# All eight weight tiles of the second product prepared in the first layer stage, with low parts on GpSimd

## The chip, the core and the metric

The kernel runs on one core of a Trainium2 chip. TensorE (PE) multiplies matrices into PSUM; VectorE (DVE), ScalarE (ACT) and GpSimd (POOL) do elementwise work; SyncE (SP) mostly issues DMAs. Each engine runs its own instructions in order, and semaphores order the engines against each other. The metric is the time of one execution on the device, in microseconds (us).

## What is computed

Attention with a learned bias, and then two feed-forward layers on its output, 2304 tokens by 512. The first layer is the one that matters here:

```python
attn = softmax(q @ k.T / 8 + bias) @ v          # 4 batches x 8 heads, 576 x 64
x = attn.transpose(0, 2, 1, 3).reshape(2304, 512)
h = x @ w_in                                     # first product, 512 -> 2048
x1 = (h * cos(h)) @ w_out                        # second product, 2048 -> 512
h2 = x1 @ w_in2
out = (max(h2, 0) + alpha * min(h2, 0)) @ w_out2
```

The weights come as 64-bit floats and are made into 32-bit floats on the chip.

## The kernel before

**Arithmetic.** A product keeps 32-bit accuracy by splitting each operand into a high part (rounded, `hi`) and a low part (`lo` = value - `hi`), and adding three products: hi by hi, hi by lo, lo by hi. So weights need a conversion (`conv`: two ScalarE copies of a 64-bit float's halves, two VectorE operations, one GpSimd addition) and a split (`split_to`: a ScalarE copy for the high part, a subtraction for the low part).

**Stages.** The bias and attention stages go through 16 pairs (two heads of one batch); `h_phase0` computes `h` and `h * cos(h)`; `o_phase(0)` the second product; `h_phase1` and `o_phase(1)` the second layer.

**Weight tiles of the first product.** `wi(0, f)` makes 16 of them (`f` 0 to 15), all in the attention stages: high and low parts on GpSimd; the first six stay on chip, the others go to memory (`w_d`) and are loaded again as `w` when `h_phase0` begins.

**Weight tiles of the second product.** It is done with seven products of half-size blocks in place of eight, so each of its eight tiles (`stage_wo(0, k)`) converts two blocks of 128 rows, forms combinations of them on VectorE (`ct`, named `wt` in the trace), and leaves four groups (`leave_w`) that serve the seven products p = 1; 5, 6; 3, 7; 2, 4. For k below `NIP` = 4 they are written into tiles that stay on chip (`wo`). For k = 4 to 7 each group is split into the tile `st` (`sw` in the trace), of which there is one buffer, and stored to memory (`w2_d`, also shown as `w_d`); `o_phase(0)` loads these as `W1[p]`. The copy of the next group has to wait until the store of the one before has landed.

**Who does what, when.** The attention's loop emits stages and counts them in `j`; a list `JOBS` of weight tiles is worked off beside it. A job starts when `j` has reached `WS0 + WSR * due`, and `due` grows by the cost of each, 1.0 for a `wi`, 3.0 for a `stage_wo`. The 16 `wi` come first, then `stage_wo(0, 4)` to `(0, 7)`; `stage_wo(0, 0)` to `(0, 3)` are done in `h_phase0`, at `H0R` = 2.6 steps for each of its units. In the attention the low parts of `split_to` are GpSimd's and the stores SP's; later the low parts are VectorE's and the stores GpSimd's. A scheduler then sets the order on each engine.

**The attention's own work.** Per pair, TensorE makes scores S; VectorE adds the bias and takes the maximum (L495); ScalarE takes exps in place (L508: `P`, and once in each pair `Pr`, for the last rows of both heads); TensorE transposes P (`T_A`, `T_B`), ScalarE and VectorE copy the transposes out of PSUM, and TensorE multiplies by v (`x_A`, `x_B`).

**The first layer stage.** `h_phase0` has 36 units, each with 24 products of 512 columns (or 48 of 256) into one of three PSUM tiles. `act1` then empties the tile: ScalarE `ta` (L818), VectorE two steps of the cosine's argument (L819, L820), ScalarE the sine (L822), VectorE the product with `h` (L823), which is the last reader of the PSUM tile.

Of the kernel before, what the change touches and what calls it, by code (L numbers as in the profile page):

```python
# [9 lines left out]
F32 = mybir.dt.float32  # L10
# [5 lines left out]
ALU = mybir.AluOpType  # L16
# [9 lines left out]
NK = NF // 2  # L26
# [11 lines left out]
HIA, LOP = 2, 1  # L38
UPB, EPB = {"D": 11, "A": 4}, 6
PBUF, BTB = 6, 10  # L40
FIRST, SIDE, SMOD, BFIRST, BRATE, SPL, WS0, WSR, PER = 4, 6, 2, 8, 2.5, 3, 28, 3.6, 1.0
SR = 2.0
NSP = 2
AHEAD = 3
# [6 lines left out]
NDIR = 6  # L51
XA, HX = 2, 300
RING, LO = 4, 3
NIP, H0R, H1R = 4, 2.6, 7.0
ORDS = ((1, 5, 6, 3, 7, 2, 4), (1, 5, 6, 3, 7, 2, 4))
GRPS = (((1,), (5, 6), (3, 7), (2, 4)), ((1,), (5, 6), (2, 3), (7, 4)))

# [16 lines left out]
def attn_mlp_kernel(ctx: ExitStack, tc: tile.TileContext, a: dict, out: bass.AP):  # L74
    nc = tc.nc
    ve, se, ge, te, sy = nc.vector, nc.scalar, nc.gpsimd, nc.tensor, nc.sync
# [97 lines left out]
    w2_d = [dr.tile([7, 128, NK, 2, 256], F32, tag=f"w2_d{i}", name=f"w2_d{i}") for i in range(2)]  # L174
    g_d = [dr.tile([NF, 128, NT], F32, tag=f"g_d{i}", name=f"g_d{i}") for i in range(2)]
    chunk = {}
    WO = {}
# [4 lines left out]
    pinned = []  # L182
# [16 lines left out]
    def hold(ins):  # L199
        if pinned:  # L200
            return behind(ins, anchor[-1]) if anchor else ins
        return behind(ins, exps[-1]) if FIRST in firsts else ins
# [42 lines left out]
    def halves_of(x):  # L245
        return x[:, 0:256], x[:, 256:512]

    def cols(x, n):
        return x.rearrange("p (n q) -> p n q", n=n)

    def split_to(hi, lo, w, eng=None):
        hold(se.activation(out=hi, in_=w, func=AF.Copy))
        yield
        hold((eng or (ve if pinned else ge)).tensor_tensor(out=lo, in0=w, in1=hi.bitcast(F32), op=ALU.subtract))
        yield

    PLACES = [{p: (g, i) for g, ps in enumerate(G) for i, p in enumerate(ps)} for G in GRPS]
# [1 line left out]
    def leave_w(layer, k, g, x):  # L259
        ps = GRPS[layer][g]  # L260
        n = len(ps)
        if (layer == 0 and k < NIP) or (layer == 1 and g < 3):
            w = WO[layer, g]
            yield from split_to(w[:, :, k, 0, :], w[:, :, k, 1, :], x)
            return
        st = wpool["t"].tile([128, 2, 2, 256], F32R, tag="st", name=f"sw{layer}_{k}_{g}")
        yield from split_to(st[:, 0:n, 0, :], st[:, 0:n, 1, :], x)
        for i, p in enumerate(ps):
            (ge if pinned else sy).dma_start(out=w2_d[layer][SLOT[p], :, k], in_=st[:, i].bitcast(F32))
        yield  # L270

    SLOT = {p: p - 1 for p in range(1, 8)}

    def stage_wo(layer, k):
        box = []
        yield from conv(layer, 2 * k, 1, box)
        yield from conv(layer, 2 * k + 1, 1, box)
        ct = wpool["t"].tile([128, 4, 256], F32, tag="ct", name=f"wt{layer}_{k}")
        sub = lambda o, u, v, op=ALU.subtract: hold(ve.tensor_tensor(out=o, in0=u, in1=v, op=op))
        c0, c1, c2, c3 = (ct[:, i] for i in range(4))  # L280
        u1, u2 = halves_of(box[0])
        v1, v2 = halves_of(box[1])
        if layer == 0:
            sub(c0, u2, v2, ALU.add)
            sub(c3, u1, u2)
            yield
            sub(c1, c0, u1)
            sub(c2, v1, c1)
            yield
            order = (cols(u1, 1), ct[:, 0:2], ct[:, 2:4], cols(box[1], 2))  # L290
        else:
            sub(c0, u2, u1)
            sub(c2, v2, u2)
            yield
            sub(c1, v2, c0)
            sub(c3, v1, c1)
            yield
            order = (cols(u1, 1), ct[:, 0:2], cols(box[1], 2), ct[:, 2:4])
        for g, x in enumerate(order):
            yield from leave_w(layer, k, g, x)  # L300
# [459 lines left out]
    W1 = {}  # L760
# [4 lines left out]
    def h_phase0():  # L765
# [5 lines left out]
        with ExitStack() as c:  # L771
# [65 lines left out]
            for f in range(NDIR, NF):  # L837
                wt[f] = wb[f - NDIR].tile([128, 2, 512], F32R, tag="w", name=f"w{f}")
                fetch(wt[f].bitcast(F32), w_d[f])
            fetch(W1[1].bitcast(F32), w2_d[0][SLOT[1], :, 4:8])  # L840
            bg.extend(stage_wo(0, k) for k in range(NIP))
            quota = 0.0
            for j, (t, f) in enumerate(units):
                ps = emit_h(t, f)
# [2 lines left out]
                if t + 1 < len(TILES):  # L847
                    with tc.high_priority(offset=XP):
# [4 lines left out]
                        if f in ((8, 12) if TILES[t][1] < TMAX else (XA + 4, XA + 6)):  # L853
                            k = 2 * (f in (12, XA + 6) and f != 8 or f == 8 and TILES[t][1] == TMAX)
# [227 lines left out]
    def h_phase1():  # L1082
        runs = [[(0, 512), (512, 1024)], [(1024, 1536), (1536, 2048)], [(2048, 2304)]]
        with ExitStack() as c:
# [6 lines left out]
            def x_prep(q):  # L1091
                x = X[q // 2][:, :, :, 2 * TS * (q % 2):2 * TS * (q % 2) + 2 * TS]
                for h in range(NCC):
                    if q < NSP:
                        ins = ge.dma_start(out=x[:, :, h].bitcast(F32), in_=x1_d[q][:, h].rearrange("l p i n -> p l (i n)"))
                        later(ins, last[0])
                        continue
                    (sy if q == 2 else ge).dma_start(out=x[:, 1, h].bitcast(F32), in_=x1_d[q][h].rearrange("p i n -> p (i n)"))
                yield
                for h in range(NCC if q >= NSP else 0):  # L1100
                    yield from split_to(x[:, 0, h], x[:, 1, h], x[:, 1, h].bitcast(F32))
                have.add(q)
# [141 lines left out]
```

## Time and profile before

| | |
|---|---|
| median of three runs | 1097.58 us (1096.16 to 1098.42) |
| the profiled execution | 1097.86 us, of which the span of its instructions 1096.0 |
| busy: TensorE, VectorE, ScalarE, GpSimd | 96%, 73%, 59%, 21% of the span |
| chain that ended last | TensorE 81%, DMA 6%, VectorE 6%, ScalarE 4%, GpSimd 1% |
| bytes moved | 216.09 MB, 197 GB/s in the mean |

The busy share is a mean over stages with different limits: which engine binds a stage is read from that stage's windows and from who waited for whom there. The chain is followed back from the last instruction, at each step to what released it.

### The profile page before, as it was taken

To read this page: it belongs to the slowest core of one execution; us is meant where nothing else is said; L and a number is where in the kernel's file an instruction comes from. 1 tells how busy PE (TensorE), PEld (TensorE's weight loads), DVE (VectorE), ACT (ScalarE), POOL (GpSimd) and SP (SyncE) were. 2 spreads that over 40 slices of the span, in tenths; PEclk is the share of its full clock that TensorE was granted. 3 is DMA by queue.
4 is the path that set the end of the run, shared out by engine and by line. 5 is a ranking of instruction groups with operands and counts; after the bars stand their busy time and mean duration, and the time that the engine had idled before them with its cause. 6 is when DMAs were issued, how large, how long until landed. Compare 5 with 4: busy or idle time off the path is not lost.

```text
span 1096.0 us, 18670 instructions
## 1 busy us (share of the span) xinstructions
PE 1055.6 (96%) x7024; PEld 891.4 (81%) x7024; DVE 802.1 (73%) x1296; ACT 642.8 (59%) x1076; POOL 225.5 (21%) x232
## 2 busy tenths in 40 slices
PE   6799999999789999999999999999999999999998
PEld 1246677777567889888899999988888889999998
DVE  7876787777675898878787777677756847777673
ACT  6996777887775565555454545466555544444442
POOL 0005675674343110010000000323222300000000
PEclk9999999999999999999999999999999999999999
DMA  8765748675448654336568172876655649554621
GB/s 322 221 171 161 220 138 270 197 218 188 154 138 304 247 195 163 135 135 227 216 205 305 47 250 70 322 263 226 221 203 185 223 164 361 158 198 130 216 73 44
DMA packets 105578, 216.09 MB, mean 197 GB/s; under 512 B 11280, under 2 KB 57104, under 8 KB 104080
## 3 DMA queue, kind: packets, MB, share of 16 engines
q1 hardware_dynamic: 75088, 154.07, 44.1%
q10 hardware_dynamic: 27968, 50.34, 12.2%
q0 software_dynamic: 2432, 10.49, 2.5%
q8 instruction: 55, 0.90, 0.4%
q14 instruction: 35, 0.29, 0.1%
HBM read 132.14 MB, written 82.72 MB: 196 GB/s over the span
## 4 chain that ended last, share of the span: by engine, by line
PE 81%; DMA 6%; DVE 6%; ACT 4%; issue 2%; POOL 1%; SPq 1%; ACTq 0%; POOLq 0%; DVEq 0%
PE h L809 18%; PE v L1139 18%; PE ob L1008 14%; PE oc L1008 9%; PE oa L1008 8%; PE S L479 5%; PE x_B L598 2%; PE T_A L573 2%; PE T_B L573 2%; DVE P L495 2%; PE x_A L598 2%; DMA w_d<-sw 1%; PE bps L142 1%; ACT be L156 1%; DMA bias_d<-be 1%
## 5 line engine op out<-in xcount | busy, mean ns | idle before, releaser
L1139 PE MATMUL v<-x,v 128*128 128x512 f32 (+1 forms) x984 | 198.0, 364 | 0.0
L1139 PEld LDWEIGHTS v<-x,v 128*128 128x128 f32 x984 | 168.5, 189 | 29.5
L809 PE MATMUL h<-xhi,w 128*128 128x512 f32 (+1 forms) x640 | 183.9, 372 | 0.0
L236 POOL TENSOR_TENSOR wc<-wc,wp 128x512 int32<-128x512 int32 x64 | 87.7, 1370 | 238.6 <-DVE wc L233 169.0
L809 PEld LDWEIGHTS h<-xhi,w 128*128 128x128 f32 x640 | 116.0, 188 | 22.1 <-PE h L809 0.4
L990 ACT ACTIVATE op<-a 128x768 fp32r<-128x768 f32 x84 | 70.5, 844 | 84.5 <-PE ob L1008 27.3
L809 PE MATMUL h<-xlo,w 128*128 128x512 f32 (+1 forms) x320 | 118.5, 370 | 0.0
L991 DVE TENSOR_TENSOR op<-a,op 128x768 fp32r<-128x768 f32 x84 | 80.1, 957 | 51.0 <-ACT op L990 48.8
L508 ACT ACTIVATE P<-P,nm 128x576 f32<-128x576 f32 x128 | 99.0, 776 | 20.9 <-DVE nm L495 20.7
L495 DVE CUSTOM_DVE_ANT_0 P<-S,bt 128x576 f32<-128x576 f32 x128 | 91.6, 751 | 26.7 <-PE S L479 17.6
L990 ACT ACTIVATE op<-b 128x768 fp32r<-128x768 f32 x84 | 70.7, 844 | 62.2 <-PE ob L1008 22.2
L991 DVE TENSOR_TENSOR op<-b,op 128x768 fp32r<-128x768 f32 x84 | 79.9, 955 | 26.5 <-ACT op L990 26.3
L1150 DVE SCALAR_TENSOR_TENSOR u<-v,asg,u 128x1024 f32<-128x1024 f32 (+2 forms) x48 | 48.0, 1013 | 39.7 <-ACT u L1149 39.3
L1008 PE MATMUL ob<-op,wo 128*128 128x384 f32 x432 | 76.4, 336 | 0.0
L818 ACT ACTIVATE ta<-h,quart 128x1024 int32<-128x1024 f32 x36 | 40.0, 1111 | 60.3 <-PE h L809 42.6
L1008 PEld LDWEIGHTS ob<-op,wo 128*128 128x128 f32 x432 | 75.1, 188 | 0.0
L809 PEld LDWEIGHTS h<-xlo,w 128*128 128x128 f32 x320 | 60.4, 189 | 11.0
L1149 ACT ACTIVATE u<-v,sgn 128x1024 f32<-128x1024 f32 (+2 forms) x48 | 43.0, 898 | 40.4 <-PE v L1139 40.3
L819 DVE SCALAR_TENSOR_TENSOR tb<-ta,h 128x1024 f32<-128x1024 int32 x36 | 43.9, 1218 | 24.8 <-ACT ta L818 24.7
L233 DVE SCALAR_TENSOR_TENSOR wc<-raw,wc 128x512 int32<-128x512 int32 x64 | 55.8, 876 | 1.3
L1008 PE MATMUL oc<-wq,op 128*128 128x256 f32 x432 | 53.3, 283 | 0.2 <-DVE op L991 0.2
L1008 PEld LDWEIGHTS oc<-wq,op 128*128 128x128 f32 x432 | 52.4, 192 | 0.7 <-DVE op L991 0.7
(154 smaller groups left out, 2066.8 us busy)
## 6 DMA issues: line engine op xcount, KB each, us to landing
a<-g_d SPq DMA_DIRECT2D x60, 384.0 KB, 4.5
g_d<-tb ACTq DMA_DIRECT2D x36, 512.0 KB, 3.1
b<-g_d SPq DMA_DIRECT2D x48, 384.0 KB, 4.7
raw<-in_wi_dram SPq DMA_DIRECT2D x32, 512.0 KB, 3.8
raw<-in_wo_dram SPq DMA_DIRECT2D x32, 512.0 KB, 4.2
g_d<-u ACTq DMA_DIRECT2D x28, 512.0 KB, 3.1
bias_d<-be SPq DMA_DIRECT2D x36, 295.5 KB, 3.3
x_d<-o ACTq DMA_DIRECT2D x20, 384.0 KB, 5.0
```

Source lines behind the costliest of these rows:

```text
L233: hold(ve.scalar_tensor_tensor(out=c, in0=raw[:, :, 1], scalar=-2 ** 31, in1=c, op0=ALU.bitwise_and, op1=ALU.bitwise_xor))
L236: ge.tensor_tensor(out=c, in0=c, in1=p, op=ALU.add)
L479: pe(te.matmul(ps[:, hf, 0:HS], lhsT=w[r, 128 * i:128 * i + 128], rhs=m[r, c0:c0 + HS], start=(j == 0), stop=(j == len(terms) - 1)))
L495: keep(2, ve.tensor_tensor_reduce(out=sn.rearrange("p (a b) -> p a b", a=2), in0=ps[:, :, 0:HS], in1=bt[hp, s].rearrange("p (a b) -> p a b ...
L508: exps.append(se.activation(out=e, in_=e, func=AF.Exp, bias=nm, scale=-1.0, accum_out=sums[n, u][:, col, 0:1]))
L809: te.matmul(ps[:, i], lhsT=w_[:, wx, w], rhs=xx[:, 0:n], start=(j == 0), stop=(j == 11))
L819: ve.scalar_tensor_tensor(out=g, in0=tt, scalar=-C1, in1=h, op0=ALU.mult, op1=ALU.add)
L990: se.activation(out=o[:, 0], in_=x, func=AF.Copy)
L991: lows.append(ve.tensor_tensor(out=o[:, 1], in0=x, in1=o[:, 0].bitcast(F32), op=ALU.subtract))
L1008: ins = te.matmul(ps[:, m], lhsT=x[:, sl] if L else w[:, sl], rhs=w if L else x, start=first, stop=kk == NK - 1 and n == 2, skip_group_che ...
L1139: ins = te.matmul(both[:, i, 0:a1 - a0], lhsT=w[:, wx, 128 * cc:128 * cc + 128], rhs=x[:, xx, cc, a0 - o:a1 - o], start=(n == 0), stop=(n ...
L1150: ve.scalar_tensor_tensor(out=g, in0=ps, scalar=asg[:, f:f + 1], in1=g, op0=ALU.mult, op1=ALU.max)
```

## The change

The four `stage_wo` jobs leave the attention's list. `h_phase0` now does all eight, 4 to 7 first, at 5.2 steps a unit. The 16 `wi` jobs are spread over the attention with 6.4 in place of 3.6. Low parts of the first layer's second product are GpSimd's, now in `h_phase0`. The group p = 1 of k = 4 to 7 is written straight into its tile on chip, so that one load goes; the other three groups still pass through `st` and memory, with their stores on GpSimd's queue.

```diff
-FIRST, SIDE, SMOD, BFIRST, BRATE, SPL, WS0, WSR, PER = 4, 6, 2, 8, 2.5, 3, 28, 3.6, 1.0
+FIRST, SIDE, SMOD, BFIRST, BRATE, SPL, WS0, WSR, PER = 4, 6, 2, 8, 2.5, 3, 28, 6.4, 1.0
...
-NIP, H0R, H1R = 4, 2.6, 7.0
+H0R, H1R = 5.2, 7.0
...
     def split_to(hi, lo, w, eng=None):
         hold(se.activation(out=hi, in_=w, func=AF.Copy))
         yield
-        hold((eng or (ve if pinned else ge)).tensor_tensor(out=lo, in0=w, in1=hi.bitcast(F32), op=ALU.subtract))
+        hold((eng or ve).tensor_tensor(out=lo, in0=w, in1=hi.bitcast(F32), op=ALU.subtract))
         yield
...
     def leave_w(layer, k, g, x):
         ps = GRPS[layer][g]
         n = len(ps)
-        if (layer == 0 and k < NIP) or (layer == 1 and g < 3):
-            w = WO[layer, g]
-            yield from split_to(w[:, :, k, 0, :], w[:, :, k, 1, :], x)
+        if (layer == 0 and (k < 4 or not g)) or (layer == 1 and g < 3):
+            w, i = (W1[1].rearrange("p (o k) t n -> p o k t n", o=1), k - 4) if not layer and k > 3 else (WO[layer, g], k)
+            yield from split_to(w[:, :, i, 0, :], w[:, :, i, 1, :], x, None if layer else ge)
             return
         st = wpool["t"].tile([128, 2, 2, 256], F32R, tag="st", name=f"sw{layer}_{k}_{g}")
-        yield from split_to(st[:, 0:n, 0, :], st[:, 0:n, 1, :], x)
+        yield from split_to(st[:, 0:n, 0, :], st[:, 0:n, 1, :], x, None if layer else ge)
         for i, p in enumerate(ps):
             (ge if pinned else sy).dma_start(out=w2_d[layer][SLOT[p], :, k], in_=st[:, i].bitcast(F32))
...
-    JOBS += [(stage_wo, (0, k), 3.0, [(0, 2 * k, 1), (0, 2 * k + 1, 1)]) for k in range(NIP, NK)]
...
-            fetch(W1[1].bitcast(F32), w2_d[0][SLOT[1], :, 4:8])
-            bg.extend(stage_wo(0, k) for k in range(NIP))
+            bg.extend(stage_wo(0, k) for k in (4, 5, 6, 7, 0, 1, 2, 3))
```

What the scheduler makes of it is seen in the order of instructions (line numbers are one or two lower in the changed kernel). ScalarE late in the attention, from the exps of the third block of the 14th pair on (`sw_k_g` is group g of second-product tile k in `st`; `wc`, `wp` are the two copies of a conversion); before:

```order
L508 ACTIVATE P_2_3997,sume_120<-P_2_3997,nm_3_3998 128x576
L558 ACTIVATE T_A<-T_A_4022 128x2x256
L508 ACTIVATE P_2_3997,sume_120<-P_2_3997,nm_7_4000 128x576
L252 ACTIVATE sw_4_2_3199<-wt_4_3065 128x2x256
L558 ACTIVATE T_A<-T_A_4038 128x2x256
L508 ACTIVATE P_3_4072,sume_120<-P_3_4072,nm_4_4073 128x576
L508 ACTIVATE P_3_4072,sume_120<-P_3_4072,nm_8_4075 128x576
L252 ACTIVATE sw_4_3_3265<-wc_9_1_3058 128x2x256
L558 ACTIVATE T_A<-L_A 128x2x256
L508 ACTIVATE P_0_4107,sume_121<-P_0_4107,nm_1_4108 128x576
```

The same place now:

```order
L507 ACTIVATE P_2_3842,sume_120<-P_2_3842,nm_3_3843 128x576
L557 ACTIVATE T_A<-T_A_3867 128x2x256
L507 ACTIVATE P_2_3842,sume_120<-P_2_3842,nm_7_3845 128x576
L557 ACTIVATE T_A<-T_A_3883 128x2x256
L507 ACTIVATE P_3_3909,sume_120<-P_3_3909,nm_4_3910 128x576
L226 ACTIVATE wc_15_0_3925<-raw_15_0_3777 128x512
L227 ACTIVATE wp_15_0_3926<-raw_15_0_3777 128x512
L226 ACTIVATE wc_8_1_4582<-raw_8_1_4580 128x512
L507 ACTIVATE P_3_3909,sume_120<-P_3_3909,nm_8_3912 128x576
L557 ACTIVATE T_A<-L_A 128x2x256
```

The copies into `sw` are gone from between the exps, and the conversion of the last `wi` tile (15) stands there, with the first step of one second-product block (8).

GpSimd in the first layer stage, from the end of tile 7 (before) on; before, only the conversions' additions are left to it:

```order
L254 TENSOR_TENSOR sw_7_2_4143<-wt_7_4044,sw_7_2_4143 128x2x256
L254 TENSOR_TENSOR sw_7_3_4148<-wc_15_1_3976,sw_7_3_4148 128x2x256
L236 TENSOR_TENSOR wc_1_1_4834<-wc_1_1_4834,wp_1_1_4835 128x512
L236 TENSOR_TENSOR wc_2_1_5066<-wc_2_1_5066,wp_2_1_5067 128x512
L236 TENSOR_TENSOR wc_3_1_5116<-wc_3_1_5116,wp_3_1_5117 128x512
```

Now, in the middle of tiles 5 and 6:

```order
L254 TENSOR_TENSOR sw_5_2_4901<-wt_5_4823,sw_5_2_4901 128x2x256
L269 DMA w_d_79<-sw_5_2_4901 128x512 x2
L236 TENSOR_TENSOR wc_12_1_4946<-wc_12_1_4946,wp_12_1_4947 128x512
L254 TENSOR_TENSOR sw_5_3_4906<-wc_11_1_4816,sw_5_3_4906 128x2x256
L254 TENSOR_TENSOR wo_1_4457<-wc_12_1_4946,wo_1_4457 128x256
L269 DMA w_d_79<-sw_5_3_4906 128x512 x2
L236 TENSOR_TENSOR wc_13_1_4996<-wc_13_1_4996,wp_13_1_4997 128x512
```

Low parts and pairs of stores stand between the additions.

ScalarE in the same stage, at its third tile of tokens (`ta` is the first step of a unit's `act1`, `tb` at L821, before L822, the sine); before:

```order
L818 ACTIVATE ta_0_5403<-h_0_5354,quart 128x1024
L790 ACTIVATE xhi_2_5609<-xlo_2_5412 128x512
L824 DMA g_d_81<-tb_14_5341 128x2x512
L790 ACTIVATE xhi_3_5612<-xlo_3_5414 128x512
L226 ACTIVATE wc_5_1_5422<-raw_5_1_5420 128x512
L227 ACTIVATE wp_5_1_5423<-raw_5_1_5420 128x512
L818 ACTIVATE ta_4_5475<-h_4_5426,quart 128x1024
L822 ACTIVATE tb_0_5404<-tb_0_5404,hpi 128x1024
L824 DMA g_d_81<-tb_0_5404 128x4x256
L818 ACTIVATE ta_8_5535<-h_8_5486,quart 128x1024
```

Now:

```order
L252 ACTIVATE sw_7_1_5260<-wt_7_5220 128x2x256
L817 ACTIVATE ta_4_5389<-h_4_5340,quart 128x1024
L821 ACTIVATE tb_0_5318<-tb_0_5318,hpi 128x1024
L823 DMA g_d_81<-tb_0_5318 128x4x256
L252 ACTIVATE sw_7_2_5265<-wt_7_5220 128x2x256
L817 ACTIVATE ta_8_5457<-h_8_5408,quart 128x1024
L821 ACTIVATE tb_4_5390<-tb_4_5390,hpi 128x1024
L226 ACTIVATE wc_0_1_5399<-raw_0_1_5397 128x512
L227 ACTIVATE wp_0_1_5400<-raw_0_1_5397 128x512
L823 DMA g_d_81<-tb_4_5390 128x4x256
L821 ACTIVATE tb_8_5458<-tb_8_5458,hpi 128x1024
L252 ACTIVATE sw_7_3_5335<-wc_15_1_5180 128x2x256
```

Three copies into the one `st` buffer stand here with one `ta` between each and the next; the first of the twelve stands after three `ta` of the stage, the last, this `sw_7_3`, after nineteen.

## Rows read from the trace of the kernel before

**Rows 1.** Busy us of each engine by window, then PEclk, DMA share, GB/s.

```profile
240.00:260.00 20.00, 20.00 (x182) 15.83 (x184) 14.87 (x38) 16.73 (x39) 13.10 (x14) 1.00 0.83 268
280.00:300.00 20.00, 15.03 (x134) 11.26 (x133) 13.24 (x34) 13.23 (x30) 6.58 (x7) 1.00 0.49 150
340.00:540.00 200.00, 199.96 (x967) 167.84 (x967) 165.13 (x186) 111.72 (x135) 20.64 (x15) 1.00 0.58 206
```

**Rows 2.** The chain that ended last, in order of time; start us, us, what.

```profile
310.15 1.28 POOL sw L254
...
339.99 122.50 PE h L809 x624
462.51 66.96 PE h L809 x288
```

**Rows 3.** Who waited for whom, whole span; us in total, times, longest us.

```profile
ACT sw L252 <- DMA w_d<-sw: 14.9, 9, 3.4
```

**Rows 4.** ScalarE's timeline, the exps of `Pr`; start us, us, what.

```profile
126.32 0.79 ACT L508 ACTIVATE Pr<-Pr,nm 128x576 f32<-128x576 f32 x1
...
145.03 0.77 ACT L508 ACTIVATE Pr<-Pr,nm 128x576 f32<-128x576 f32 x1
...
161.75 0.76 ACT L508 ACTIVATE Pr<-Pr,nm 128x576 f32<-128x576 f32 x1
...
242.15 0.77 ACT L508 ACTIVATE Pr<-Pr,nm 128x576 f32<-128x576 f32 x1
...
257.40 0.77 ACT L508 ACTIVATE Pr<-Pr,nm 128x576 f32<-128x576 f32 x1
...
316.39 0.76 ACT L508 ACTIVATE Pr<-Pr,nm 128x576 f32<-128x576 f32 x1
```

**Rows 5.** VectorE's timeline at 333.6 us; in brackets the idle time before.

```profile
333.63 0.43 DVE L279 TENSOR_TENSOR wt<-wc 128x256 f32<-128x256 f32 x1 [4.50 <-POOL sw L254]
```

**Rows 6.** Instructions by form; count | busy us, mean ns | idle before.

```profile
L233 DVE SCALAR_TENSOR_TENSOR wc<-raw,wc 128x512 int32<-128x512 int32 x64 | 55.8, 876 | 1.3
...
L820 DVE SCALAR_TENSOR_TENSOR tb<-ta,tb 128x1024 f32<-128x1024 int32 x36 | 45.2, 1256 | 0.1
L823 DVE TENSOR_TENSOR tb<-h,tb 128x1024 f32<-128x1024 f32 x36 | 43.9, 1219 | 9.9 <-ACT tb L822 9.9
L819 DVE SCALAR_TENSOR_TENSOR tb<-ta,h 128x1024 f32<-128x1024 int32 x36 | 43.9, 1218 | 24.8 <-ACT ta L818 24.7
...
L822 ACT ACTIVATE tb<-tb,hpi 128x1024 f32<-128x1024 f32 x36 | 41.2, 1145 | 18.3 <-DVE tb L820 18.2
L818 ACT ACTIVATE ta<-h,quart 128x1024 int32<-128x1024 f32 x36 | 40.0, 1111 | 60.3 <-PE h L809 42.6 <-DVE tb L820 16.6 <-DVE wc L232 0.9
...
L232 DVE TENSOR_SCALAR wc<-wc 128x512 int32<-128x512 int32 x48 | 26.9, 561 | 6.5 <-ACT wc L226 6.3
...
L254 POOL TENSOR_TENSOR sw<-wt,sw 128x512 fp32r<-128x512 f32 x8 | 10.3, 1285 | 36.7 <-ACT sw L252 36.7
L279 DVE TENSOR_TENSOR wt<-wc,wt 128x256 f32<-128x256 f32 x24 | 10.1, 420 | 7.7 <-POOL wc L236 7.5
L252 ACT ACTIVATE sw<-wt 128x512 fp32r<-128x512 f32 x16 | 10.0, 627 | 6.6 <-DMA w_d<-sw 6.3 <-DVE wt L279 0.2
...
L254 DVE TENSOR_TENSOR wo<-wt,wo 128x512 fp32r<-128x512 f32 x8 | 5.5, 684 | 0.0
```

**Rows 7.** Line 269, the stores of `sw`; ns min/median/max, then landing of all.

```profile
L269 POOL DMA_DIRECT2D w_d<-sw x16: 542/560/822, 741.8 to 883.6; - x16
...
DMA to landing us min/median/max: 2.0/4.3/10.5
```

**Rows 8.** DMA issues by line; KB each, median us from issue to landing.

```profile
w_d<-sw POOLq DMA_DIRECT2D x16, 256.0 KB, 5.0
```

**Rows 9.** Timelines of GpSimd and VectorE at 371 to 374 us.

```profile
371.47 1.30 POOL L254 TENSOR_TENSOR sw<-wt,sw 128x512 fp32r<-128x512 f32 x1 [11.15 <-ACT sw L252]
...
372.14 1.71 DVE L820 SCALAR_TENSOR_TENSOR tb<-ta,tb 128x1024 f32<-128x1024 int32 x1
```

## The prediction

> **What bounds the kernel now.** I read the busy time by stretch first. In the first layer stage (340 to 540 us) TensorE is busy 199.96 of 200 us, while VectorE has 165.1, ScalarE 111.7 and GpSimd 20.6; late in the attention stages, at 280 to 300 us, TensorE is busy 15.0 of 20, against 20.0 at 240 to 260 [rows 1]. So the one stage is bound by TensorE and the other, at its end, is not. The chain that ended last names what it waits for there: a GpSimd subtraction `sw` at 310.15 us and, after the attention, TensorE's `h` products, which run from 339.99 us for 122.50 + 66.96 us without a break [rows 2]. The waits say why `sw` is on the chain: ScalarE, in order, stood 14.9 us before nine copies into `sw`, because the one `st` buffer was still being stored to memory [rows 3]; behind such a copy stand the exps and the copies of P's transposes.
>
> ScalarE's timeline then gives a clock for the attention: the exp of `Pr` comes once in each pair. From the fifth pair to the last it takes 316.39 - 126.32 = 190.07 us for eleven pairs [rows 4]. The seven pairs between 145.03 and 257.40 us, which carry ten `wi` tiles and no second-product tile, take 112.37 us, 16.05 each; the last three, with the second-product tiles, take 58.99 us, 19.66 each; the first of the eleven, with three `wi` tiles, takes 18.71 us [rows 4].
>
> **The change, part by part.**
>
> *Attention.* Four second-product tiles leave it, and the `wi` tiles are spread out: by the order, fourteen of them lie in the eleven pairs, never more than two in one (1.27 a pair; the seven pairs just read had 1.43), and one conversion of a second-product tile. So I price all eleven pairs as the seven: 11 x 16.05 = 176.6 us against 190.07, **-13.5 us**; of this 10.8 come from the last three pairs and 2.7 from the first. Bounds: the quickest of the seven, from 242.15 to 257.40 with one `wi`, took 15.25, which gives 167.8 and -22.3 us; the first of them, with two `wi`, took 16.72, which gives 183.9 and -6.2 us [rows 4].
>
> *The tail, from the last `Pr` at 316.39 to the unbroken `h` products at 339.99 us.* VectorE stood 4.50 us behind GpSimd's `sw` there [rows 5], with the last copies of T_B queued behind it. Most of it was covered: by the order TensorE had the 24 products of unit 0 to do meanwhile, which it must do in either kernel. I take **-1.5 us**, between 0 and -4.5.
>
> *First layer stage.* It gets four tiles more, over some 30 of its 36 units. A unit is 189.46 us / 35 = 5.41 us of TensorE [rows 2]. TensorE hides the new work if the others keep within that.
> VectorE: 165.1/200 of a unit is 4.47 us [rows 1]. A tile adds 2 x (0.56 + 0.88) + 4 x 0.42 = 4.56 us; the four tiles that stood here give up their low parts, 3 x 0.684 and one half as wide, say 2.4 us each [rows 6]. 4 x (4.56 - 2.4) = 8.6 us over 30 units is 0.29: 4.76 of 5.41.
> ScalarE: 111.7/200 is 3.02 us; a tile adds eight instructions, none longer than the 1.15 of the sine: at most 1.2 us a unit, 4.2 of 5.41.
> GpSimd: 16 additions and 32 low parts of at most 1.29 [rows 6], and 24 DMA issues of 0.56 [rows 7]: 75 of 162 us.
> None of the three becomes the bound by its sum. If TensorE's cover were gone, VectorE's 8.6 us would be the price.
>
> *The new wait.* The copies into `st` now stand between ScalarE's `ta` and sine, and the stores stand on GpSimd's queue, not SP's. One link from copy to copy is copy 0.63, low part 1.29 [rows 6], first issue 0.56 [rows 7], second landed after 5.0 [rows 8]: 7.5 us, with handovers some 7.7. The order has eleven links between the first such copy (after three `ta`) and the last (after nineteen): 16 units, 86.6 us of TensorE, against 11 x 7.7 = 85 us. That is close, but it holds. Two links of one unit each follow at the end, so single copies will wait some 2 to 4 us, with `ta` and sine queued behind them, then VectorE, then the release of a PSUM tile. With three PSUM tiles TensorE needs one back two units after it finished with it, 10.8 us; the five instructions that free it take 1.11 + 1.22 + 1.26 + 1.15 + 1.22 = 5.96 us [rows 6]. That leaves 4.9 us for such waits. GpSimd's additions for the next tile stand behind the low part that waits, and VectorE's combinations behind those; they are late next, within the same 4.9 us. I take **+1 us**, between 0 and the rivals below.
>
> *At nothing:* the load of the p=1 tile that goes, and 24 stores and eight weight loads more in this stage, whose DMA share was 0.58 [rows 1]. SP loses the `sw` stores ahead of its loads of `w`, so these come no later. The last part of the last tile is copied after 32 of 36 `ta`, four units before the second product: nothing is late there.
>
> *Sum:* -13.5 - 1.5 + 1 = -14.0 us. The profiled execution took 1097.86 us (span 1096.0), so 1083.9; the median of the runs is 0.3 lower: **1084 us**.
>
> **What speaks against it: the lock.** While GpSimd's low part ran, from 371.47 to 372.77 us, VectorE's second step of the cosine, begun at 372.14, took 1.71 us [rows 9], where its kind needs about 1.22: VectorE waits for GpSimd. The Trainium skill (SBUF — State Buffer, "Who interferes with whom") says that a VectorE instruction with two SBUF inputs and a GpSimd instruction that reads SBUF lock each other out for a whole instruction, and that GpSimd's DMA issues can starve likewise. By that rule this row is what one would expect.
> How often it happens is read from rows. All 36 of these steps together average 1.256 where the first step, which has one operand in PSUM, has 1.218 [rows 6]: 36 x 0.038 = 1.4 us of delay for 15 GpSimd instructions [rows 1], 0.09 us each. The change makes them 48, which would cost 4.4 us, and VectorE has (5.41 - 4.76) x 30 = 20 us to spare.
>
> **The rivals.**
> 1. *The store link is slower than TensorE, and the kernel ends slower.* At some 9.5 us a link, 11 links take 104.5 us, 18 more than 86.6, and beyond the 4.9 us of slack the rest, 13, eats the gain; at 10 us the loss is 18.5 and the time 1097.9 - 15 + 18.5 = 1101 us. For it: `sw` stores have taken up to 10.5 us to land [rows 7]. Against it: their median is 4.3 [rows 7], on GpSimd's queue 5.0 [rows 8]. Chance 0.08.
> 2. *The lock.* At 0.65 us (half a low part) for each of the 48, VectorE gets 31 us more against 20 to spare: +11 us, about 1094; the point at which it begins to cost is 0.42 us each, that at which it turns the sign 0.7. For it: the single delay of 0.5 us; against it: the mean of 0.09. Chance 0.06.
> 3. *The attention gains less.* The last three pairs fall only to 16.72, the first not at all, the tail gives nothing: -8.8 + 1, 1090 us. For it: some pairs with two `wi` tiles did take that. Chance 0.13.
> 4. *It gains more:* all pairs near 15.25 and the tail in full, about 1075 us. Chance 0.05.
> That the tiles don't leave the attention is excluded: by the order no `sw` stands there.
>
> **How the numbers follow.** The forecast (1079 to 1088 us on its own) has 0.68. The range, 1078 to 1094 us, adds most of rivals 2 and 3 and leaves out rival 1 and most of 4. A measurement of this kernel tells about 0.2%, 2.2 us, from no change. Faster: forecast, 3, 4 and a part of 2, 0.88; same 0.04, from the milder ends of 1 and 2; slower 0.08.
>
> **What would show it.** Right: `Pr` comes every 15.5 to 16.5 us to the end of the attention, ScalarE's waits before `sw` in the attention are gone, and the `h` products begin some 15 us earlier and still fill TensorE at 5.4 us a unit. Wrong: gaps of TensorE inside the first layer stage, released by `ta`, the sine or a PSUM tile, with copies into `sw` waiting for stores (rival 1) or steps of the cosine well over 1.26 us in the mean (rival 2); or pairs that stay above 17 us with no `sw` left, which would make my reading of the stall wrong.

## The result, and the profile after

The changed kernel takes 1086.45 us (1085.97 to 1091.23), the kernel before 1098.00 beside it: a ratio of 0.9903, interval 0.9882 to 0.9925. The profiled execution took 1086.3 us, span 1084.5 against 1096.0. So 11.5 us were gained where 14.0 were forecast. (Lines are one or two lower now: the exps are L507, `ta` L817, the cosine's steps L818 and L819, the sine L821, the product with `h` L822, the `h` products L808; `op` at L989 forms the second product's first operands, `oa` is its first product.)

ScalarE's timeline gives the attention's clock as in [rows 4]:

```profile
126.17 0.77 ACT L507 ACTIVATE Pr<-Pr,nm 128x576 f32<-128x576 f32 x1
...
141.94 0.77 ACT L507 ACTIVATE Pr<-Pr,nm 128x576 f32<-128x576 f32 x1
...
252.38 0.77 ACT L507 ACTIVATE Pr<-Pr,nm 128x576 f32<-128x576 f32 x1
...
300.27 0.78 ACT L507 ACTIVATE Pr<-Pr,nm 128x576 f32<-128x576 f32 x1
```

Eleven pairs take 300.27 - 126.17 = 174.10 us in place of 190.07: 15.97 gained. The last three take 47.89 in place of 58.99, the first 15.77 in place of 18.71. The chain that ended last, as in [rows 2]:

```profile
323.31 33.42 PE h L808 x144
356.86 33.59 PE h L808 x144
...
537.79 4.25 PE oc L1006 x23
```

From the last `Pr` to the unbroken `h` products it is 323.31 - 300.27 = 23.04 us (before 23.60), so the first layer stage begins 16.7 us earlier. But TensorE's chain of `h` breaks off after 67 us of 201, and the piece of `oc` that began at 548.71 us in the chain of the kernel before now stands at 537.79, only 10.9 earlier: **5.8 us are lost in the first layer stage**. The windows show where (columns as in [rows 1]):

```profile
280.00:300.00 20.00, 19.53 (x172) 15.37 (x169) 15.38 (x42) 15.57 (x38) 6.60 (x8) 1.00 0.26 88
340.00:540.00 200.00, 194.54 (x950) 163.21 (x949) 176.12 (x190) 121.05 (x154) 75.69 (x70) 1.00 0.62 215
440.00:460.00 20.00, 17.87 (x76) 13.64 (x74) 19.93 (x25) 13.14 (x20) 7.97 (x7) 1.00 0.46 148
...
500.00:520.00 20.00, 18.38 (x80) 14.66 (x79) 18.40 (x18) 11.92 (x16) 6.79 (x5) 1.00 0.88 340
```

TensorE lacks 2.1 us at 440 to 460 us, where VectorE is busy 19.93 of 20, and 1.6 us at 500 to 520, where VectorE is busy 18.40. Who waited for whom, whole span; us in total, times, longest us:

```profile
ACT sw L252 <- DMA w_d<-sw: 7.3, 4, 3.3
PE h L808 <- DVE tb L822: 4.8, 6, 1.7
```

The copies into `sw` waited for stores four times only, 7.3 us in all [rows 3]; TensorE waited for VectorE's last reading of a PSUM tile, 4.8 us in six waits. The timelines at the longest of these, of TensorE (in brackets the idle time before),

```profile
453.92 0.48 PE L808 MATMUL h<-xhi,w 128*128 128x512 f32 x1 [1.69 <-DVE tb L822]
```

of GpSimd,

```profile
453.43 1.27 POOL L236 TENSOR_TENSOR wc<-wc,wp 128x512 int32<-128x512 int32 x1 [0.78 <-ACT wp L227]
454.67 0.92 POOL L254 TENSOR_TENSOR wo<-wc,wo 128x256 fp32r<-128x256 f32 x1
```

and of VectorE:

```profile
452.56 1.21 DVE L822 TENSOR_TENSOR tb<-h,tb 128x1024 f32<-128x1024 f32 x1
453.69 1.30 DVE L279 TENSOR_TENSOR wt<-wc 128x256 f32<-128x256 f32 x1
454.92 1.75 DVE L819 SCALAR_TENSOR_TENSOR tb<-ta,tb 128x1024 f32<-128x1024 int32 x1
```

Beside GpSimd's two instructions a combination of 0.42 us takes 1.30 and a cosine step of 1.22 takes 1.75, as in [rows 9]. So three explanations stood against each other: **A**, GpSimd's low parts delay VectorE; **B**, VectorE's own added work; **C**, the link from one copy into `sw` to the next, through the store.

### The profile page after: what moved, and what is told of

The parts are those of the page before. It is cut to its first block, busy times and chain, and to the rows that moved or that the text cites. A ratio compares the mean times of both kernels' runs of the same rounds, so it can differ in the third digit from the quotient of the medians.

```text
span 1084.5 us, 18708 instructions
## 1 busy us (share of the span) xinstructions
PE 1052.3 (97%) x7024; PEld 890.9 (82%) x7024; DVE 800.9 (74%) x1280; ACT 643.9 (59%) x1076; POOL 262.0 (24%) x272
## 4 chain that ended last, share of the span: by engine, by line
PE 78%; DVE 10%; ACT 4%; DMA 4%; issue 3%; POOL 1%; SPq 0%; ACTq 0%; DVEq 0%; POOLq 0%
PE v L1137 18%; PE ob L1006 14%; PE oc L1006 9%; PE oa L1006 9%; PE h L808 7%; PE S L478 6%; PE x_B L597 3%; PE T_A L572 3%; PE x_A L597 2%; DVE tb L818 2%; DVE tb L819 2%; PE T_B L572 2%; PE bps L142 2%; ACT be L156 1%; DVE tb L822 1%
## 5 line engine op out<-in xcount | busy, mean ns | idle before, releaser
L808 PE MATMUL h<-xhi,w 128*128 128x512 f32 (+1 forms) x640 | 185.2, 372 | 4.9 <-DVE tb L822 4.8
L808 PEld LDWEIGHTS h<-xhi,w 128*128 128x128 f32 x640 | 115.9, 188 | 29.0 <-PE h L808 4.1
L808 PE MATMUL h<-xlo,w 128*128 128x512 f32 (+1 forms) x320 | 118.6, 370 | 0.0
L989 DVE TENSOR_TENSOR op<-a,op 128x768 fp32r<-128x768 f32 x84 | 80.0, 957 | 50.5 <-ACT op L988 48.4
L507 ACT ACTIVATE P<-P,nm 128x576 f32<-128x576 f32 x128 | 99.2, 778 | 21.9 <-DVE nm L494 21.4
L989 DVE TENSOR_TENSOR op<-b,op 128x768 fp32r<-128x768 f32 x84 | 80.8, 968 | 28.2 <-ACT op L988 28.0
L808 PEld LDWEIGHTS h<-xlo,w 128*128 128x128 f32 x320 | 60.4, 189 | 10.8
L817 ACT ACTIVATE ta<-h,quart 128x1024 int32<-128x1024 f32 x36 | 40.0, 1112 | 32.3 <-DVE tb L819 20.1
L821 ACT ACTIVATE tb<-tb,hpi 128x1024 f32<-128x1024 f32 x36 | 41.4, 1149 | 27.3 <-DVE tb L819 27.2
L233 DVE SCALAR_TENSOR_TENSOR wc<-raw,wc 128x512 int32<-128x512 int32 x64 | 55.0, 864 | 1.2
L818 DVE SCALAR_TENSOR_TENSOR tb<-ta,h 128x1024 f32<-128x1024 int32 x36 | 43.7, 1215 | 14.7 <-ACT ta L817 14.6
```

Of the source, the lines that this page charges most:

```text
L233: hold(ve.scalar_tensor_tensor(out=c, in0=raw[:, :, 1], scalar=-2 ** 31, in1=c, op0=ALU.bitwise_and, op1=ALU.bitwise_xor))
L507: exps.append(se.activation(out=e, in_=e, func=AF.Exp, bias=nm, scale=-1.0, accum_out=sums[n, u][:, col, 0:1]))
L808: te.matmul(ps[:, i], lhsT=w_[:, wx, w], rhs=xx[:, 0:n], start=(j == 0), stop=(j == 11))
L818: ve.scalar_tensor_tensor(out=g, in0=tt, scalar=-C1, in1=h, op0=ALU.mult, op1=ALU.add)
L989: lows.append(ve.tensor_tensor(out=o[:, 1], in0=x, in1=o[:, 0].bitcast(F32), op=ALU.subtract))
```

## The experiments

A measure for all of them is the stage's length, from the unbroken `h` products to `oa`: 534.74 - 339.99 = 194.75 us before, 524.31 - 323.31 = 201.00 after, 6.25 lost. (The first three expectations count to the piece of `oc` instead: 208.72 before, 214.48 after.) A stage's length comes from one profiled execution, and the scheduler makes a new order for each kernel, so a difference of a microsecond between two variants is not laid to one instruction. Ratios are to the kernel before; the changed kernel's interval, 0.9882 to 0.9925, overlaps those of all variants here but 5, 7 and 8, that of 4 by a hair.

### 1. Low parts without GpSimd, without VectorE

```diff
-        hold((eng or ve).tensor_tensor(out=lo, in0=w, in1=hi.bitcast(F32), op=ALU.subtract))
+        hold(se.activation(out=lo, in_=w, func=AF.Copy, scale=2.0 ** -12) if eng is ge and pinned else ...)
```

> The changed kernel, with the 32 low parts of the second product's weights in the first layer stage made by ScalarE as a scaled copy of the value; the subtraction itself is left out, so the output isn't the product's, but every tile is written, stored and read as before. GpSimd keeps only the additions and the DMA issues. In the changed kernel the stage from the unbroken h products to the second product takes 537.79 - 323.31 = 214.48 us, in the kernel before 548.71 - 339.99 = 208.72: 5.8 us are lost there. Theory A (GpSimd's low parts hold up VectorE's operations with two operands in SBUF): the stage falls back to 209 to 210.5 us and the time to about 1081 us, a ratio to before of 0.985; TensorE's gaps at 440 to 480 us are gone. Theory B (VectorE's own work of the eight tiles is too much in places): VectorE's instructions are the same, so the stage stays at 213 to 215 us, 1086 us, ratio 0.990. Theory C (the copies into sw wait for the stores, behind them ta and the sine): a link gets only some 0.6 us shorter, 212 to 214 us.

Measured: 1082.08 us, ratio 0.9862 (0.9833 to 0.9891); the stage takes 520.60 - 323.01 = 197.59 us, 3.4 less than in the changed kernel (to `oc` 211.07, just above what A said). VectorE runs the same 191 instructions in it. The window of the whole stage, of the kernel before and of the changed kernel,

```profile
339.99:534.74 194.75, 194.71 (x938) 162.59 (x937) 160.54 (x181) 108.40 (x132) 20.64 (x15) 1.00 0.57 205
323.31:524.31 201.00, 196.09 (x936) 162.11 (x936) 176.66 (x191) 123.42 (x157) 79.63 (x73) 1.00 0.64 225
```

then of this one:

```profile
323.01:520.60 197.59, 195.33 (x937) 162.50 (x936) 164.43 (x191) 136.65 (x189) 36.63 (x41) 1.00 0.65 229
```

With the low parts gone from GpSimd VectorE's busy time for the same instructions is 176.66 - 164.43 = 12.2 us shorter: that was delay, 0.38 us for each of the 32 low parts. By form, the changed kernel,

```profile
L819 DVE SCALAR_TENSOR_TENSOR tb<-ta,tb 128x1024 f32<-128x1024 int32 x35 | 45.1, 1289 | 0.2
L818 DVE SCALAR_TENSOR_TENSOR tb<-ta,h 128x1024 f32<-128x1024 int32 x35 | 42.5, 1215 | 13.5 <-ACT ta L817 13.3
...
L279 DVE TENSOR_TENSOR wt<-wc,wt 128x256 f32<-128x256 f32 x8 | 7.8, 971 | 0.1
```

and this one:

```profile
L818 DVE SCALAR_TENSOR_TENSOR tb<-ta,h 128x1024 f32<-128x1024 int32 x35 | 42.6, 1218 | 21.6 <-ACT ta L817 21.5
L819 DVE SCALAR_TENSOR_TENSOR tb<-ta,tb 128x1024 f32<-128x1024 int32 x35 | 42.6, 1218 | 0.1
...
L279 DVE TENSOR_TENSOR wt<-wc,wt 128x256 f32<-128x256 f32 x8 | 3.4, 421 | 0.1
```

The combinations fall from 0.971 to 0.421 us, the cosine's second step from 1.289 to 1.218; the first step, which has an operand in PSUM, is the same in both. The Trainium skill (SBUF — State Buffer, "Who interferes with whom") has only VectorE instructions with two SBUF inputs, or in certain modes, wait for GpSimd; these rows agree. A is shown as a part: it stands for 3.4 of 6.25 us. TensorE is busy 39.81 of 40 us at 440 to 480, as A said. But 2.8 us stay, more than A left room for: 1.4 of them a gap at 500 to 520 us (18.63 of 20 busy), the rest short gaps and products that take 0.6 us longer in sum (195.33 us busy against 194.71 before).

### 2. Low parts on VectorE

```diff
-            yield from split_to(w[:, :, i, 0, :], w[:, :, i, 1, :], x, None if layer else ge)
+            yield from split_to(w[:, :, i, 0, :], w[:, :, i, 1, :], x)
...
-        yield from split_to(st[:, 0:n, 0, :], st[:, 0:n, 1, :], x, None if layer else ge)
+        yield from split_to(st[:, 0:n, 0, :], st[:, 0:n, 1, :], x)
```

> The changed kernel, with the 32 low parts on VectorE, as before the change. VectorE gets 24 x 0.684 + 8 x 0.42 = 19.8 us more of work, GpSimd has no low part left. Theory A (GpSimd's low parts hold up VectorE): what VectorE gets in work it saves in delays, if these are near 0.6 us for each of 32 instructions; the stage stays within 2 us of 214.5, the time within 1084 to 1088 us, and the mean of the cosine's second step falls back to 1.25 us. Theory B (the sum of VectorE's work): the stage gets longer by most of the 19.8 us, at least 8: 1094 us or more. Theory C (the store link): a link gets 0.6 us shorter, so the stage gets shorter by 1 to 4 us, 1083 us.

Measured: 1083.52 us, 0.987 (0.9837 to 0.9902), stage 197.90 us (to `oc` 211.56). VectorE is busy 179.82 of 197.90 us, 3 more than in the changed kernel, and yet TensorE loses 3 us less. The cosine's second step has a mean of 1.242 us, as A said. That is against B, and better than A's "nothing"; C names this time too, and the next experiment decides on C. I read it so: work that the order provides for costs TensorE less than delays that it doesn't; no run here tests that by itself. This is the fastest kernel here in its median that computes the whole product (1 leaves the subtraction out); its interval overlaps that of the changed kernel.

### 3. Stores on SP's queue

```diff
-            (ge if pinned else sy).dma_start(out=w2_d[layer][SLOT[p], :, k], in_=st[:, i].bitcast(F32))
+            (ge if layer else sy).dma_start(out=w2_d[layer][SLOT[p], :, k], in_=st[:, i].bitcast(F32))
```

> The changed kernel, with the 24 pairs of stores of sw in the first layer stage issued on SP's queue, where they stood in the attention before the change, in place of GpSimd's. Theory A and theory B: GpSimd's issues, 48 of some 0.56 us, don't bound anything; the stage stays at 213 to 215.5 us, the time at 1085 to 1088 us. Theory C (the store link, or the issues that stand between GpSimd's additions): the stage falls by 3 us or more, to 1083 us or less.

Measured: 1087.95 us, 0.992 (0.989 to 0.995), stage 200.60 us (to `oc` 215.77). No copy into `sw` of this stage waits for a store any more, and the stage is as long as without this edit: C falls.

### 4. The `wi` tiles bunched as before

```diff
-... WS0, WSR, PER = 4, 6, 2, 8, 2.5, 3, 28, 6.4, 1.0
+... WS0, WSR, PER = 4, 6, 2, 8, 2.5, 3, 28, 3.6, 1.0
```

> The changed kernel, with the wi tiles bunched as before the change (a step of 3.6 in place of 6.4), so that of the change in the attention only the removal of the four second-product tiles is left. My reading of before: the tiles that left gave 10.8 of 13.5 us, the spreading 2.7 us. By it the exps of Pr take some 3 us more from the fifth pair to the last (177 in place of 174.10 us) and the time is 1088 to 1090 us. Rival: the spreading does most of it, since any tile beside a pair costs: 6 us or more, 1092 us or above. Second rival: the spreading gives nothing, 1086 us.

Measured: 1090.61 us, 0.9944 (0.9924 to 0.9964). The eleven pairs take 303.13 - 125.84 = 177.29 us. So taking the four tiles out gives 190.07 - 177.29 = 12.8 us, spreading the `wi` 177.29 - 174.10 = 3.2.

### 5. The side work faster

```diff
-H0R, H1R = 5.2, 7.0
+H0R, H1R = 6.4, 7.0
```

> The changed kernel, with 6.4 in place of 5.2 steps of the side work a unit, so that the eight tiles are done some four units sooner and no step of them stands beside the second product's first combinations (op), which begin at 505.74 us in the changed kernel; GpSimd keeps the low parts. In the changed kernel the time from the unbroken h products to the first product of the second product (oa) is 524.31 - 323.31 = 201.00 us, before 194.75: 6.25 lost, of which 2.8 stayed when GpSimd's low parts were gone, all of it at 500 to 524 us. Theory A2 (two separate losses, one by the delays from GpSimd's low parts at 440 to 480 us, one by the late end of the side work): the second goes, 198 to 199 us and the time about 1083.5. Rival (what counts is how dense the side work and the delays lie): the same delays in fewer units cost more, 202 us or above, 1087 or more.

Measured: 1093.15 us, 0.9962 (0.9949 to 0.9975), stage 206.30 us: the rival. Its windows:

```profile
440.00:460.00 20.00, 16.24 (x69) 13.04 (x68) 19.92 (x21) 13.94 (x21) 11.18 (x8) 0.96 0.43 141
460.00:480.00 20.00, 18.38 (x75) 14.18 (x74) 19.93 (x22) 11.78 (x17) 12.88 (x10) 0.95 0.52 154
...
500.00:520.00 20.00, 20.00 (x89) 16.44 (x88) 16.93 (x16) 11.19 (x12) 0.00 (x0) 1.00 0.83 283
520.00:540.00 20.00, 20.00 (x102) 18.05 (x101) 15.29 (x15) 8.40 (x9) 0.00 (x0) 1.00 0.46 174
```

The loss at the end is gone, as A2 said: TensorE is full from 500 to 540 us. But VectorE is full for 40 us at 440 to 480, and there more is lost than at the end is won. (The granted clock fell there too, to 0.96 and 0.95 in the mean of these windows, so part of the loss is the clock's.)

### 6. Faster, with the later low parts on VectorE

To the edit of 5 comes, for the tiles written on chip:

```diff
-            yield from split_to(w[:, :, i, 0, :], w[:, :, i, 1, :], x, None if layer else ge)
+            yield from split_to(w[:, :, i, 0, :], w[:, :, i, 1, :], x, None if layer or k < 4 else ge)
```

> The changed kernel with 6.4 steps a unit, and the low parts of tiles k = 0 to 3 on VectorE, where they were before the change; those of k = 4 to 7 stay on GpSimd. Theory A2: the losses at 440 to 480 us and at 500 to 524 us both go; what is left is what GpSimd's first sixteen low parts cost, none in the changed kernel's 327 to 430 us: 195 to 197 us to oa, the time 1079 to 1082 us. Rival (VectorE's sum of work, which gets 9.9 us more): 199 us or more, 1084 or above.

Measured: 1090.73 us, 0.9936 (0.9919 to 0.9953), stage 204.08 us. The end is free again; the middle isn't, and A2 falls: the stage is longer than its rival's 199 us. A part of it is the clock's: after a gap of 3.00 us TensorE ran at a lower granted clock (third number from the end of a row):

```profile
454.00:456.00 2.00, 0.00 (x0) 0.00 (x0) 2.00 (x3) 2.00 (x4) 0.00 (x0) 0.90 0.00 0
456.00:458.00 2.00, 1.44 (x4) 1.18 (x5) 2.00 (x3) 1.21 (x3) 0.00 (x0) 0.50 0.34 125
458.00:460.00 2.00, 2.00 (x6) 1.62 (x5) 2.00 (x6) 1.82 (x2) 0.00 (x0) 0.50 0.37 141
460.00:462.00 2.00, 2.00 (x6) 1.52 (x6) 2.00 (x4) 0.49 (x1) 1.27 (x1) 0.50 0.50 70
```

### 7. The kernel before, with only its low parts moved to GpSimd

```diff
-            yield from split_to(w[:, :, k, 0, :], w[:, :, k, 1, :], x)
+            yield from split_to(w[:, :, k, 0, :], w[:, :, k, 1, :], x, None if layer else ge)
```

> The kernel before, with only the low parts of its four tiles in the first layer stage moved from VectorE to GpSimd: sixteen instructions, and nothing else of the change. VectorE loses 12 x 0.684 + 4 x 0.416 = 9.9 us of work there. Theory A (each low part on GpSimd delays VectorE by some 0.4 us, as 12.7 us for 32 in the changed kernel against the one with low parts on ScalarE): VectorE's operations L233, L279 and L820 get longer by 5 to 8 us together; as VectorE had 34 us spare in 194.75, TensorE waits little: 194.7 to 196 us to oa, the time 1097 to 1099 us. Rival (a low part on GpSimd costs what the prediction took, 0.09 us): L233 and L279 keep their means of 0.711 and 0.42 us. Second rival (a low part on GpSimd costs TensorE by its length, through the copies that wait for it): 197 us or more, 1100 us.

Measured: 1100.53 us, 1.0028 (1.0013 to 1.0042): slower by some 3 us, with 9.9 us less work on VectorE. The profiled execution is the slowest of twelve (1104.02 us). By form, from 345 us to the end of the stage:

```profile
L820 DVE SCALAR_TENSOR_TENSOR tb<-ta,tb 128x1024 f32<-128x1024 int32 x35 | 47.1, 1347 | 0.3
...
L794 DVE TENSOR_TENSOR xlo<-xlo,xhi 128x512 fp32r<-128x512 f32 x12 | 9.0, 774 | 0.0
...
L232 DVE TENSOR_SCALAR wc<-wc 128x512 int32<-128x512 int32 x10 | 5.3, 528 | 0.1
...
L279 DVE TENSOR_TENSOR wt<-wc,wt 128x256 f32<-128x256 f32 x5 | 3.0, 603 | 0.1
...
L794 DVE TENSOR_TENSOR xlo<-xlo,xhi 128x256 fp32r<-128x256 f32 x4 | 2.7, 686 | 0.0
```

In the kernel before the means were 1.257, 0.706, 0.419, 0.421 and 0.419 us: 3.2 + 0.8 + 1.1 + 0.9 + 1.1 = 7.1 us more, less 0.2 in L233, which got shorter (0.687 for 0.711). That is 6.8 us of delay for sixteen low parts, 0.43 each, near the price in 1. TensorE waited for VectorE at 393.90 and 401.77 us, 1.50 and 2.04 us, and after the second wait it ran at the lower granted clock (0.50) for a while:

```profile
401.77 0.47 PE L809 MATMUL h<-xhi,w 128*128 128x512 f32 x1 [2.04 <-DVE tb L823]
```

```profile
404.00:406.00 2.00, 2.00 (x6) 1.52 (x6) 1.60 (x2) 1.41 (x2) 1.29 (x1) 0.50 0.26 52
```

Counted from the end of the last `x_B` product, as in the other kernels, the stage takes 542.51 - 342.15 = 200.36 us, 5.6 more than before: 3.5 are the two waits, the rest products that took longer, those at the lower clock among them. The second rival had named this time as well, by copies that wait for a low part; ScalarE waited so twice, 1.8 us in all, at 496 and 507 us, long after the two gaps. So the low parts' move alone makes the kernel before a little slower, though VectorE has room in the mean; that the two gaps come from the delays is read from one execution.

### 8. The kernel before, with a second staging buffer in the attention

```diff
-        st = wpool["t"].tile([128, 2, 2, 256], F32R, tag="st", name=f"sw{layer}_{k}_{g}")
+        st = wpool["t2" if not pinned and g % 2 == 0 else "t"].tile([128, 2, 2, 256], F32R, tag="st", name=...)
...
-            v_p = c.enter_context(tc.tile_pool(name="vp", bufs=FIRST + 1))
+            v_p = c.enter_context(tc.tile_pool(name="vp", bufs=FIRST))
...
+                        wpool["t2"] = c.enter_context(tc.tile_pool(name="wt2", bufs=1, **right))
```

> The kernel before, with a second buffer st for every other group of the second-product tiles in the attention (one buffer less for v), so that a copy need not wait for the store just before it; all work stays where it was. If the last three pairs (58.99 us, 19.66 each) were long because of the waits before the copies into sw, they fall to some 17 us each and the time to 1088 to 1091 us; ScalarE's waits for the stores (14.9 us) fall below 5. If they were long because of the tiles' work itself on VectorE, ScalarE and GpSimd, they stay above 18.5 each, and the time stays at 1095 to 1098 us.

Measured: 1096.15 us, 0.999 (0.9979 to 1.0001), no change that can be told. The wait that stood at 14.9 us [rows 3],

```profile
ACT sw L252 <- DMA w_d<-sw: 0.5, 2, 0.3
```

and the last three pairs:

```profile
257.65:274.58 16.93, 16.64 (x150) 12.54 (x149) 12.72 (x34) 13.64 (x32) 7.07 (x9) 1.00 0.46 150
274.58:295.20 20.62, 15.59 (x142) 11.84 (x138) 17.62 (x42) 16.84 (x38) 12.17 (x12) 1.00 0.64 212
295.20:314.94 19.74, 17.17 (x156) 12.92 (x156) 16.53 (x38) 16.73 (x38) 10.54 (x11) 1.00 0.74 224
```

With the waits gone the three pairs take 57.29 us in place of 58.99, and two of them still 20.62 and 19.74: for the most part it was the tiles' work beside the pair, not the store, that made them long. The buffer that `v` gave up cost nothing that shows: the `Pr` of the thirteenth pair comes at 257.65 us, before at 257.40. Which of VectorE, ScalarE and GpSimd it is was not settled.

### 9 to 11. The pace, by place

In 9 the pace dips where the last token tile is split (first line below); 10 is the same with the edit of 2; 11 is a slower pace throughout.

```diff
-                quota += H0R
+                quota += 2.6 if 20 < j < 25 else 5.8
...
-H0R, H1R = 5.2, 7.0
+H0R, H1R = 4.7, 7.0
```

> The changed kernel, with the pace of the side work changed only in place: 2.6 steps a unit in units 21 to 24, where the split of the last token tile (four xlo on VectorE, 442 to 460 us in the changed kernel) stands, and 5.8 in the others in place of 5.2. Low parts stay on GpSimd. Theory A3 (VectorE has room in the mean, but not where the tiles' work, GpSimd's delays and the split meet): the gaps at 440 to 462 us go, some 3 us; those at 500 to 524 us stay; 197 to 199 us from the unbroken h products to oa in place of 201.0, the time 1083 to 1084.5 us. Rival (VectorE's work and delays are too much for the stage as a whole): the same loss turns up in other units, 200.5 to 203 us, 1086 to 1089 us.

> The same pace (2.6 in units 21 to 24, 5.8 elsewhere), with all low parts on VectorE, so without GpSimd's delays. With low parts on VectorE at an even pace it took 197.9 us to oa and 1083.5 in all, with gaps of 1.1 us at 460 to 480 us and 1.4 at 500 to 520. Theory A3: the first of these goes, 196.5 us, 1082 us. Rival (the higher pace of the other units fills VectorE there): gaps before 440 us, 199 us or more, 1085 us.

> The changed kernel at 4.7 in place of 5.2 steps a unit: less of the side work in each unit, but the last tile is done some four units later, just ahead of the second product. At 6.4 steps a unit it took 1093.2 us, 6.7 more than at 5.2. If density alone decides, the gaps at 440 to 480 us shrink to under 1 us, and the time falls to about 1083 us. If the late end costs what the density saves, the first product of the second layer half (oa) or its first combinations (op) wait, with gaps after 500 us of 5 us or more, and the time stays at 1086 us or rises.

Measured: 9, 1089.88 us, 0.9937 (0.9917 to 0.9958), stage 203.04; 10, 1087.06, 0.9914 (0.9896 to 0.9933), stage 201.83; 11, 1089.41, 0.9934 (0.9916 to 0.9952). In 9 the window of 440 to 460 us is full, as A3 said, but the loss turns up after it:

```profile
440.00:460.00 20.00, 20.00 (x88) 16.22 (x88) 18.35 (x22) 12.67 (x18) 8.28 (x8) 1.00 0.39 138
460.00:480.00 20.00, 17.89 (x76) 13.86 (x75) 19.52 (x20) 11.28 (x17) 12.81 (x10) 1.00 0.54 150
480.00:500.00 20.00, 16.64 (x71) 12.87 (x70) 17.94 (x20) 13.10 (x17) 7.03 (x7) 1.00 0.46 163
```

A3 falls: it is not one crowded place. In 10 the time is nearer the rival's (its 199 us or more hold), but not its place: TensorE has no gap before 480 us, and lacks 1.9 and 2.6 us in the next two windows. In 11 (where "oa" is the second product's first product) the windows are full to 500 us, and the late end costs more:

```profile
440.00:500.00 60.00, 60.00 (x260) 48.29 (x259) 55.69 (x60) 38.10 (x49) 26.45 (x20) 1.00 0.52 175
...
520.00:540.00 20.00, 13.80 (x63) 13.40 (x64) 19.96 (x22) 11.75 (x15) 7.30 (x4) 0.74 0.77 257
```

TensorE's gaps there:

```profile
523.58 0.69 PE L1006 MATMUL oa<-op,wo 128*128 128x384 f32 x1 [4.43 <-ACT op L988]
526.88 10.79 PE L1006 MATMUL oa<-op,wo 128*128 128x384 f32 x47 [2.61 <-DVE op L989]
```

With 5 this is the answer: at 6.4 steps a unit VectorE is too full, at 4.7 the tiles are done too late, at 5.2 some of both is paid. How much the slower pace loses is less sure than that it gains nothing: its interval overlaps that of the changed kernel a little, and the lower clock after the gap (0.74 in the mean of the last window) adds to its loss, as in 10 at 500 to 520 us (0.91).

### 12. Only the later low parts on VectorE

The edit of 6, at the changed kernel's own pace.

> The changed kernel at its own pace (5.2), with the low parts of tiles k = 0 to 3 on VectorE and those of k = 4 to 7 on GpSimd. In the changed kernel TensorE had no gap before 440 us, where the tiles 4 to 7 are made, so GpSimd's delays should cost nothing there: if it is the delays in the second half that cost, this kernel does as well as the one with all low parts on VectorE: 197.5 to 198.5 us from the unbroken h products to oa, 1083 to 1084.5 us. If the delays of the first half count too, since they push the side work later, it lies between the two, 199 to 200.5 us and 1085 to 1086 us. If VectorE's sum of work decides, it is better than the one with all low parts on VectorE: 196 us, 1082.

Measured: 1087.82 us, 0.9908 (0.989 to 0.9926), stage 522.75 - 322.26 = 200.49 us, at the edge of the second case in the stage, and in the time no better than the changed kernel. Its window of the gap:

```profile
440.00:460.00 20.00, 17.11 (x72) 13.30 (x73) 19.93 (x29) 13.80 (x20) 2.86 (x2) 1.00 0.43 135
```

GpSimd does only 2.86 us there, and TensorE still lacks 2.9. In 2, which differs only in the low parts of the first half, it is busy 20.00 of these 20 us. So, as far as two orders can be compared (2.6 us between the two stages), the delays of the first half count, though no gap of TensorE over 0.3 us stands where they happen; that they push VectorE's work on to where its room ends is how I read it, and is not shown.

## Why the prediction was right, and where it was off

The forecast of 1084 us in 1078 to 1094 held; the sign and most of the size came from the attention.

**Attention: -13.5 forecast, -15.97 measured**, inside its bounds. The two parts, 10.8 and 2.7, measured 12.8 and 3.2 (experiment 4). But the reason given, that ScalarE's copies stood before the one `st` buffer, was wrong for the most part: without those waits the last three pairs gained 1.7 us and the time nothing that can be told (8). The number survived because it was read from pairs with and without tiles, not from the wait.

**Tail: -1.5 forecast, -0.56 measured.**

**First layer stage: +1 forecast, +6.25 to `oa` (+5.8 to `oc`) measured.** This is the term that was mis-sized. Its first step, "0.09 us each", was too low: a low part on GpSimd cost VectorE 0.38 us (1), 0.43 in another kernel (7). The 0.09 counted the cosine's second step alone, and the delays fall on the combinations, the conversions and the splits of `x` as well (0.971 for 0.421 us). It was also shared among 15 instructions of which 11 were additions: beside the four low parts two of these steps took 1.76 and 1.71 us in place of 1.22, which is 1.0 of the 1.4 us. Its second step, "20 us to spare", failed more: rival 2 took 0.42 us for each of 48 instructions to be free, and here 12.2 us, well within 20, cost TensorE 3.4, since that room was a mean and VectorE is full at 440 to 460 us. VectorE's own work had been taken too high: four tiles more were to add 8.6 us, and 1 shows 164.43 - 160.54 = 3.9 with the low parts elsewhere; with the delays it was 176.66 - 160.54 = 16.1. Of the other 2.8 us 1.4 are the late end beside `op`, of which the prediction said "nothing is late there"; 5 and 11 show it by moving it.

One reading was wrong without harm: 189.46 us hold 34 units and not 35 (624 + 288 products, 24 in thirty of the units and 48 of half the width in four), so a unit is 5.57 us and not 5.41. VectorE's share of a unit grows with it, and its room stays 20 us.

**New wait and rival 1:** the stores landed 3.1 us after their issue in the median, where 5.0 had been taken; `sw` copies waited 7.3 us in all, and taking the waits away gave nothing (3).

Together: -15.97 - 0.56 - 0.15 (the fifth `Pr` came that much earlier) + 5.8 - 0.6 in the rest of the kernel, -11.5 us. Open stays why VectorE with more work in 2 costs TensorE less than with delays.

## What to carry to other kernels

An instruction moved to GpSimd to relieve VectorE was paid for here in VectorE's delays. Count what all kinds of VectorE's instructions beside it lose, and not one kind: some 0.4 us of delay for each 0.42 to 0.68 us of work moved away went with a slower kernel (7), though VectorE had less to do in sum. Work hidden beside a bound engine needs room in each stretch and must end before the next stage starts; where neither a faster nor a slower pace gains, look for less work or fewer delays and not for another pace. A wait on the chain is a cause only once taking it away has moved the time.

## What the runs showed of the hardware

GpSimd's side is delayed too: the low parts `sw<-wt` of 1.285 us [rows 6] averaged 1.703 in the changed kernel's stage, as far as the profile times GpSimd:

```profile
L254 POOL TENSOR_TENSOR sw<-wt,sw 128x512 fp32r<-128x512 f32 x8 | 13.6, 1703 | 26.3 <-ACT sw L252 21.6 <-DVE wc L232 4.7
```

And a gap of TensorE can cost more than its length: after 3.00 us without a product (6) the granted clock stood at 0.50, the lower level of 1.2 GHz, for six us, with six products in two us in place of ten. The gap's length alone doesn't decide it. After the 1.69 us of the changed kernel and after 2.55 us in 12 the clock stayed at 1.00, while it fell to 0.50 after 2.04 us in 7 and after 2.11 us in 10. Of 12,

```profile
453.81 0.47 PE L808 MATMUL h<-xhi,w 128*128 128x512 f32 x1 [2.55 <-DVE tb L822]
```

and of 10:

```profile
513.24 0.47 PE L808 MATMUL h<-xhi,w 128*128 128x512 f32 x1 [2.11 <-DVE tb L822]
```

```profile
514.00:516.00 2.00, 2.00 (x6) 1.52 (x6) 0.74 (x2) 1.66 (x2) 0.00 (x0) 0.50 0.77 290
```

What else decides it stays open here.
